# Forward transform of a Fourier and feed-forward kernel: the first stage with the input as weights on quarters of the array, the second from SBUF on row halves

## The chip, the core and the metric

The kernel runs on one core of a Trainium2 chip. The metric is the device time of one execution in microseconds (us). Engines are named as in the profile: PE (matrix engine; PEld its weight loads), DVE and ACT (the two that read PSUM), POOL, and SP, which here only issues transfers. Operands live in SBUF (128 rows), products in eight PSUM banks of 512 float32 columns, inputs and spilled tiles in DRAM (HBM).

## The reference

Two batches of 3008 positions with 256 features pass through a transform along the positions, one complex linear layer with soft shrinkage, the transform back, and two feed-forward layers. The change lies in `rfft` alone; what follows `irfft` is named as far as it shares engines with it.

```python
X = np.fft.rfft(x, axis=1)                  # x: 2 x 3008 x 256
Yr = Xr @ w_r - Xi @ w_i + b_r
Yi = Xr @ w_i + Xi @ w_r + b_i              # then soft shrinkage by 0.01
y = np.fft.irfft(Y, n=x.shape[1], axis=1)
h = x @ w_in                                # x: y as 6016 x 256; 2048 wide
x = (h * np.clip(h + 3.0, 0.0, 6.0) / 6.0) @ w_out
out = (silu(x @ w_gate) * (x @ w_val)) @ w_out2   # 1536 wide
```

## The kernel before

3008 is split into 47 x 64. The first stage (`pre`, L324) takes transforms of 47 points over positions 64 apart; only 24 of the 47 results are wanted, each with a real and an imaginary part (48 numbers). The second stage (`s2`, L398) takes transforms of 64 points, four of the 24 groups at a time: a block (b, Q) is batch b and group four Q = 0..5. ORDER (L490) lists the twelve blocks, batch 0 first, and p counts them; batch 1 begins at p = 6.

**First stage before.** x lies in eight rooms of 94 used rows (two neighbouring positions times 47, padded to 96, spread over 128 rows from the second room on, the rest set to zero), 2048 columns each. A table `fwd1_sb` of 96 columns stands as weights, and `pre(n)` streams two times 512 columns of a room past it, n = 0..7 for batch 0 and 8..15 for batch 1; ACT and DVE each copy one result (L341, L343) to SBUF. From there it is written to DRAM (`Bd`, eight transfers on POOL's queue, one on ACT's, the others on SP's), and `load_q` (L388) reads it back with (part, position) on the rows as z, one transfer of 512 KB for each block, three buffers.

**Second stage before.** For each block and each half dh of the 256 features, `s2` multiplies four times: weights z (128 x 128), 128 moving columns of the table m (L405). `S(p)` is the pair of these halves; ACT and DVE make from each a high part, a low part, and the sum of the parts the same way (L411 to L419).

**The order.** `seq` (L510 to L531) is a hand-written list of steps; every engine works through its own instructions in that order. It begins with `prepare` (constants, the linear layer's weights `lin`, split into high and low parts during `pre` 6 to 10 by the steps of `amid`), goes on with `pre` 0 to 12, S(0) and `pre` 13, and then runs over p: L(p), the linear layer of block p, in two halves `ln` (L436) of one L456 and 18 products each; S(p+1) ahead; A(p-1), the first stage back (`ia`, L474, products on row halves of the array, L481), whose result POOL's queue writes to `Cd`. `pre` 14 and 15 stand in p = 1 and 2. Each half of L(1) to L(7) also does one step of `conv1` (L206), which turns 64-bit weights into high and low parts on ACT and DVE, with one load of 256 KB on SP's queue. At p = 8 `post` (L587) computes the last stage back for the first tokens, on quarters of the array (L584: 48 rows, 64 columns of weights, up to 47 moving columns), and from there on `unit` (L658), the first feed-forward layer, stands between the pieces of L, S and A. What comes after p = 11 is feed-forward work.

At the start four products of zeros (L271) on quarters of the array run before the first data has come. `load_x` (L244) and `load_m` (L384) put their transfers on SP's queue, which issues in order: a transfer that waits for its buffer holds up what stands behind it.

## Time and profile before

| what | us |
|---|---|
| median of 3 runs | 1136.46 |
| range of the runs | 1136.12 to 1137.76 |
| the profiled execution | 1135.67 |
| span within it (first to last instruction) | 1133.9 |
| PE busy in the span | 1124.4 |
| DVE busy | 913.4 |
| ACT busy | 779.3 |
| POOL busy | 48.5 |

Busy time is the time in which an instruction of the engine is under way; instructions of one engine overlap in it, so the distance from one start to the next says what one costs in a dense row. The chain that ended last is followed back from the last instruction, at each step to what released it. A float32 product of PE stands in the trace as two instructions, a product of rounded float32 (fp32r) as one.

### The profile page before, as it was taken

To read this page: it belongs to the slowest core of one execution; us is meant where nothing else is said; L and a number is where in the kernel's file an instruction comes from. 1 tells how busy PE (TensorE), PEld (TensorE's weight loads), DVE (VectorE), ACT (ScalarE), POOL (GpSimd) and SP (SyncE) were. 2 spreads that over 40 slices of the span, in tenths; PEclk is the share of its full clock that TensorE was granted. 3 is DMA by queue.
4 is the path that set the end of the run, shared out by engine and by line. 5 is a ranking of instruction groups with operands and counts; after the bars stand their busy time and mean duration, and the time that the engine had idled before them with its cause. 6 is when DMAs were issued, how large, how long until landed. Compare 5 with 4: busy or idle time off the path is not lost.

```text
span 1133.9 us, 18058 instructions
## 1 busy us (share of the span) xinstructions
PE 1124.4 (99%) x6576; PEld 979.9 (86%) x6576; DVE 913.4 (81%) x1629; ACT 779.3 (69%) x1432; POOL 48.5 (4%) x79
## 2 busy tenths in 40 slices
PE   9999999999999999999999999999999999999998
PEld 3898888888888888888899888888888888888997
DVE  5688996899999999999988777777777777777665
ACT  3677876688788788787787666666666666666655
POOL 4000004500000000000000000000000000000000
PEclk9999999999999999999999999999999999999999
DMA  8997534964473664554543544644644644644552
GB/s 304 335 317 229 182 97 146 297 240 172 135 252 110 197 223 153 183 200 149 209 177 126 195 166 167 241 167 168 241 167 168 241 167 168 237 168 167 208 205 75
DMA packets 70185, 219.65 MB, mean 194 GB/s; under 512 B 6688, under 2 KB 30272, under 8 KB 58368
## 3 DMA queue, kind: packets, MB, share of 16 engines
q1 hardware_dynamic: 67280, 208.76, 53.3%
q0 software_dynamic: 2496, 9.05, 2.1%
q8 instruction: 52, 0.85, 0.3%
q10 hardware_dynamic: 320, 0.69, 0.2%
q14 instruction: 37, 0.30, 0.1%
HBM read 172.07 MB, written 46.40 MB: 193 GB/s over the span
## 4 chain that ended last, share of the span: by engine, by line
PE 86%; DVE 8%; ACT 4%; issue 2%; DMA 1%; SPq 0%; DVEq 0%; ACTq 0%
PE acc L136 11%; PE acc L138 11%; PE acc L137 11%; PE P L945 8%; PE P L947 8%; PE P L946 8%; PE Tb L947 4%; PE Tb L945 4%; PE Tb L946 4%; PE p L339 2%; PE Q L945 2%; PE Q L947 2%; PE Q L946 2%; DVE r L993 2%; DVE gated L141 1%
## 5 line engine op out<-in xcount | busy, mean ns | idle before, releaser
L1002 ACT COPY hold<-P 128x512 f32<-128x512 f32 (+1 forms) x224 | 128.4, 573 | 57.3 <-PE P L947 55.8
L624 ACT CAST gated<-r 128x512 fp32r<-128x512 f32 (+1 forms) x160 | 98.4, 615 | 65.1 <-DVE r L993 63.6
L141 DVE TENSOR_TENSOR gated<-s,gated 128x512 fp32r<-128x512 f32 (+1 forms) x144 | 97.5, 677 | 49.9 <-ACT gated L1129 49.7
L141 DVE TENSOR_TENSOR gated<-r,gated 128x512 fp32r<-128x512 f32 (+1 forms) x160 | 108.1, 676 | 21.8 <-ACT gated L624 17.3
L136 PE MATMUL acc<-gated,w_o 128*128 128x512 f32 (+1 forms) x320 | 120.4, 376 | 0.0
L137 PE MATMUL acc<-gated,w_o 128*128 128x512 f32 (+1 forms) x320 | 119.6, 374 | 0.0
L138 PE MATMUL acc<-gated,w_o 128*128 128x512 f32 (+1 forms) x320 | 119.6, 374 | 0.0
L997 DVE TENSOR_TENSOR hold<-Q,hold 128x512 f32<-128x512 f32 (+1 forms) x112 | 75.9, 678 | 43.4 <-ACT hold L1002 41.8
L138 PE MATMUL acc<-gated,slot 128*128 128x512 f32 (+1 forms) x288 | 108.1, 375 | 0.0
L136 PE MATMUL acc<-gated,slot 128*128 128x512 f32 (+1 forms) x288 | 108.0, 375 | 0.1
L137 PE MATMUL acc<-gated,slot 128*128 128x512 f32 (+1 forms) x288 | 107.9, 375 | 0.0
L997 DVE TENSOR_TENSOR hold<-P,hold 128x512 f32<-128x512 f32 (+1 forms) x112 | 75.8, 677 | 33.6 <-PE P L947 33.6
L1169 ACT ACTIVATE s<-hold 128x512 f32<-128x512 f32 (+1 forms) x72 | 45.0, 624 | 81.0 <-DVE hold L997 81.0
L989 ACT ACTIVATE r<-hold,consts 128x512 f32<-128x512 f32 (+1 forms) x120 | 85.7, 714 | 14.4 <-DVE hold L997 12.4
L945 PE MATMUL P<-xo,slot 128*128 128x512 f32 (+1 forms) x240 | 90.2, 376 | 1.7 <-DVE hold L997 1.2
L1129 ACT CAST gated<-s 128x512 fp32r<-128x512 f32 (+1 forms) x144 | 87.8, 610 | 4.4 <-DVE s L1184 4.2
L947 PE MATMUL P<-xo,slot 128*128 128x512 f32 (+1 forms) x240 | 88.8, 370 | 0.0
L946 PE MATMUL P<-xo,slot 128*128 128x512 f32 (+1 forms) x240 | 88.8, 370 | 0.0
L997 DVE TENSOR_TENSOR hold<-Tb,hold 128x512 f32<-128x512 f32 (+1 forms) x112 | 75.9, 678 | 14.2 <-PE Tb L947 10.4
L993 DVE SCALAR_TENSOR_TENSOR r<-r,hold 128x512 f32<-128x512 f32 (+1 forms) x120 | 81.0, 675 | 2.5 <-ACT r L989 1.6
L1174 ACT ACTIVATE s<-hold 128x512 f32<-128x512 f32 (+1 forms) x72 | 45.0, 625 | 45.2 <-DVE hold L997 45.2
L1002 ACT COPY hold<-Tb 128x512 f32<-128x512 f32 (+1 forms) x112 | 65.2, 582 | 4.0
(190 smaller groups left out, 2847.1 us busy)
## 6 DMA issues: line engine op xcount, KB each, us to landing
slot<-Wd SPq DMA_DIRECT2D x72, 1152.0 KB
slot<-Sd SPq DMA_DIRECT2D x40, 896.0 KB
st<-in_w SPq DMA_DIRECT2D x68, 256.0 KB
Wd<-slot SPq DMA_DIRECT2D x12, 1152.0 KB
z<-Bd SPq DMA_DIRECT2D x12, 512.0 KB
Cd<-cs POOLq DMA_DIRECT2D x12, 512.0 KB, 3.4
Xd<-x SPq DMA_DIRECT2D x20, 256.0 KB
raw<-Xd SPq DMA_DIRECT2D x5, 1024.0 KB
```

What stands on the lines that cost most here:

```text
L136: nc.tensor.matmul(o, wl, xh, start=start, stop=False)
L137: nc.tensor.matmul(o, wh, xh, start=False, stop=False)
L138: nc.tensor.matmul(o, wh, xl, start=False, stop=stop)
L141: nc.vector.tensor_tensor(out=o, in0=full, in1=hi.bitcast(F32), op=ALU.subtract)
L624: nc.scalar.copy(hi[:, :n], g[:, :n])
L945: nc.tensor.matmul(o, wl, hi, start=start, stop=False, skip_group_check=not start)
L946: nc.tensor.matmul(o, wh, lo, start=False, stop=False, skip_group_check=not start)
L947: nc.tensor.matmul(o, wh, hi, start=False, stop=True, skip_group_check=not start)
L993: nc.vector.scalar_tensor_tensor(out=r[:, :n], in0=r[:, :n], scalar=6.0, in1=x[:, :n], op0=ALU.min, op1=ALU.mult)
L997: nc.vector.tensor_tensor(out=h, in0=x[:, :n], in1=c, op=ALU.add)
L1002: nc.scalar.copy(c, x[:, :n])
L1129: nc.scalar.copy(hi[:, :nb], t[:, :nb])
```

## The change

In `pre` the input itself is now the weights: for each feature, half and position block, 64 columns of x (47 rows) are loaded into one quarter of the array, and the table `fwd1_sb` (47 x 48) streams past. Four quarters take turns, two PSUM tiles collect eight features each (results 8 columns apart), and one copy of 384 columns on ACT and one on DVE move them to z in SBUF, which holds a whole batch and has one buffer. The result already has (half, position) on the rows, so the way through DRAM (`Bd`, `load_q`, `write_second`, `group`) goes. `s2` multiplies on row halves, 64 rows for each dh, twice as many products, real and imaginary part added up in PSUM; the table m has its 64 rows twice and twice the columns, in two buffers instead of three. All eight `pre` of batch 0 stand at the start, followed by S(0) and S(1); those of batch 1 stand in p = 4 and 5. x comes in four rooms a batch with 48 rows for each row half (47 and one of zeros), so the memsets of the rooms go; batch 1's rooms are loaded at the ends of p = 0 to 3. `lin` moves from POOL's queue to SP's. Four more products of zeros, 320 columns wide, stand at the start. From p = 8 on two units stand at the end of a step that were on both sides of S's halves.

The diff, cut where the code before shows what goes:

```diff
-    fwd2 = np.zeros((NG, 2, 2, NJ, 2, K2))
+    fwd2 = np.zeros((NG, 2, NJ, 2, 2, K2))
...
-    fwd2 = fwd2.reshape(NG, 128, 128).transpose(1, 0, 2).reshape(128, NG * 128)
+    fwd2 = fwd2.reshape(GC, K2, 128).transpose(1, 0, 2).reshape(K2, GC * 128)
+    fwd2 = np.concatenate([fwd2, fwd2])
...
-    both = np.zeros((128, 2 * GW))
-    mixed = fwd1.reshape(QP, NG // 4, 16).transpose(0, 2, 1).reshape(QP, GW)
-    both[:QP, :GW] = mixed
-    both[::2, GW:], both[1::4, GW:] = mixed[:64], mixed[64:]
-    inv2 = np.zeros((128, QP))
-    inv2[:48, :N1] = inv2[64:112, :N1] = f.transpose(2, 1, 0).reshape(48, N1)
-    out = {"fwd1": both, "inv2": inv2, "fwd2": fwd2, "inv1": inv1}
+    fwd1, inv2 = np.zeros((128, 64)), np.zeros((128, 96))
+    for r in (0, 64):
+        fwd1[r : r + N1, :GC] = f.reshape(N1, GC)
+        inv2[r : r + GC, :N1] = f.transpose(2, 1, 0).reshape(GC, N1)
...
-    Bd = [dram.tile([16 if n < NQ else GW, NJ * DIM], F32, name=f"Bd{n}") for n in range(NQ + 1)]
...
-    NT = NJ // 4
-    TC = 4 * DIM
-    room = {}
+    NT, ND = 8, 8
+    TC = 2 * ND * K2
 
     def ring4(name):
-        return ap_.tile([128, 4 * DIM], F32, tag="bc", name=name, bufs=4)
-
-    def load_x(k):
...
-    room[5] = xs_p.tile([128, 3 * TC], F32, tag="gs", name="room5", bufs=1)[:, : 2 * TC]
-    room[6], room[7] = room[0], room[1]
+        return ap_.tile([128, 4 * DIM], F32, tag="bc", name=name, bufs=2)
+
+    first = w1p.tile([128, NT * TC], F32, tag="w1_o", name="first", bufs=1)
+    room = {(0, k): first[:, 2 * k * TC : 2 * (k + 1) * TC] for k in range(4)}
+
+    def load_x(b, k, c=slice(0, 2 * TC)):
+        for r in range(2):
+            nc.sync.dma_start(room[b, k][64 * r : 64 * r + GC, c], x[b, k, r, :, c])
+
+    for c in (slice(0, TC // 2), slice(TC // 2, TC), slice(TC, 2 * TC)):
+        load_x(0, 0, c)
+    nc.scalar.dma_start(fwd1_sb, fwd1)
 
     p = [psf[0]([128, 512], f"p0_{n}") for n in range(2)]
-    for r, c, n in ((0, 0, 0), (64, 64, 0), (0, 64, 1), (64, 0, 1)):
-        nc.tensor.matmul(p[n][c : c + 64], zeros[r : r + 64, :64], zeros[r : r + 64], start=True, stop=True,
-                         tile_position=(r, c))
+    for n in (512, 320):
+        for r, c in ((0, 0), (64, 64), (0, 64), (64, 0)):
+            nc.tensor.matmul(p[r // 64][c : c + 64, :n], zeros[r : r + 64, :64], zeros[r : r + 64, :n], start=True,
+                             stop=True, tile_position=(r, c))
...
-        lin_st = ap_.tile([128, 2, 2, DIM], F32, tag="z", name="lin_st", bufs=3)
+        lin_st = ring4("lin_st").rearrange("p (k a b) -> p k a b", k=2, a=2)
         b_st = spread("b_st")
-        nc.gpsimd.dma_start(lin_st, lin)
+        load_x(0, 1)
+        nc.sync.dma_start(lin_st, lin)
+        load_x(0, 2)
+        load_x(0, 3)
+        load_m(0, 0)
         nc.gpsimd.dma_start(b_st[:64], bias)
-        for h in range(2):
-            nc.gpsimd.memset(room[5][:, h * TC : (h + 1) * TC], 0.0)
-        load_x(5)
-        load_m(0, 0)
...
         amid.update({
-            6: [lambda: mixed(ALU.subtract), lambda: hi(2, 0)], 7: [lambda: mixed(ALU.add), lambda: hi(0, 2)],
-            8: [lambda: lo(2, 0), lambda: shifts(0)], 9: [lambda: lo(0, 2), lambda: hi(1, 3)],
-            10: [lambda: lo(1, 3), lambda: shifts(1)]})
+            4: [lambda: mixed(ALU.subtract), lambda: hi(2, 0)], 5: [lambda: mixed(ALU.add), lambda: hi(0, 2)],
+            6: [lambda: lo(2, 0), lambda: hi(1, 3), lambda: shifts(0)],
+            7: [lambda: lo(0, 2), lambda: lo(1, 3), lambda: shifts(1)]})
 
...
-    first = w1p.tile([128, NT * TC], F32, tag="w1_o", name="first", bufs=1)
-    second = w1p.tile([128, 5 * TC], F32, tag="w1_g", name="second", bufs=1)
-
-    def pre(n):
-        sent()
-        b, i = divmod(n, NT)
+    def pre(b, i):
+        src = room[b, i // 2][:, i % 2 * TC : (i % 2 + 1) * TC]
+        if i == 0:
+            z_t[b] = ap_.tile([128, GC, 128], F32, tag="z", name=f"z{b}", bufs=1)
+        p = [psf[0]([128, 512], f"p1_{b}_{i}_{r}") for r in range(2)]
+        for n in range(ND):
+            for r, c in ((0, 0), (1, 1), (0, 1), (1, 0)):
+                k, e = slice(64 * r, 64 * r + N1), slice(64 * c, 64 * c + 64)
+                at = 128 * n + 64 * c
+                nc.tensor.matmul(p[r][e, n : n + ND * (GC - 1) + 1 : ND], src[k, at : at + 64], fwd1_sb[k, :GC],
+                                 start=True, stop=True, tile_position=(64 * r, 64 * c))
+        for r, copy in enumerate((nc.scalar.copy, nc.vector.tensor_copy)):
+            at = 64 * r + ND * i
+            copy(z_t[b][:, :, at : at + ND], p[r][:, : ND * GC].rearrange("p (a n) -> p a n", n=ND))
         if b == 0:
-            o = first[:GW, i * TC : (i + 1) * TC]
-        elif i < 4:
-            o = second[:GW, i * TC : (i + 1) * TC]
...
-
-    bview = [t.rearrange("(g w) (j d) -> (w j) g d", w=4, j=NJ) for t in Bd]
+            for g in amid.pop(i, ()):
+                g()
+
...
     def load_m(b, Q):
         if (b, Q) not in m_t:
-            m_t[b, Q] = table("m", fwd2, Q, f"m{b}_{Q}", 3)
-
-    def load_q(b, Q):
...
-            nc.tensor.matmul(p[:, g, :], z_t[b, Q][:, g, dh * 128 : (dh + 1) * 128], m_t[b, Q][:, g, :],
-                             start=True, stop=True)
+            m_t[b, Q] = table("m", fwd2, Q, 8, f"m{b}_{Q}")
+
+    def s2(b, Q):
+        flush()
+        t = ap_.tile([128, 2, 2, 3, 4 * K2], F32R, tag="X", name=f"X{b}_{Q}", bufs=2)
+        X[b, Q] = [t[:, k] for k in range(2)]
+        p = [psf[0]([128, 4, 128], f"p2_{b}_{Q}_{dh}") for dh in range(2)]
+        for i in range(8):
+            for dh in range(2):
+                r = slice(64 * dh, 64 * dh + 64)
+                nc.tensor.matmul(p[dh][:, i // 2], z_t[b][r, 8 * Q + i], m_t[b, Q][r, i], start=i % 2 == 0,
+                                 stop=i % 2 == 1, tile_position=(64 * dh, 0))
+        for dh in range(2):
+            evict(b, Q, dh, p[dh])
+
+    def evict(b, Q, dh, p):
...
-    def ahead(p):
-        if p < len(ORDER):
-            load_q(*ORDER[p])
-
     def S(p):
-        def first():
-            ahead(p + 1)
-            s2(*ORDER[p], 0)
-        return [first, lambda: s2(*ORDER[p], 1)] if p < len(ORDER) else []
+        def both():
+            if p + 1 < len(ORDER):
+                load_m(*ORDER[p + 1])
+            s2(*ORDER[p])
+        return [both] if p < len(ORDER) else []
 
...
-    P = [lambda n=n: pre(n) for n in range(NB * NT)]
-    seq = [prepare] + P[:NT] + [lambda: load_q(0, 0)] + P[NT : NT + 1]
-    seq += [lambda: group(1, nc.scalar)] + P[NT + 1 : NT + 2] + [lambda: load_q(0, 1)]
-    seq += P[NT + 2 : NT + 5] + S(0) + P[NT + 5 : NT + 6]
-    rest = P[NT + 6 :]
+    P = [[lambda b=b, i=i: pre(b, i) for i in range(NT)] for b in range(NB)]
+
+    def load_next(k):
+        if k == 0:
+            t = w1p.tile([128, 5 * TC], F32, tag="w1_g", name="second", bufs=1)
+            room.update({(1, i): t[:, 2 * i * TC : 2 * (i + 1) * TC] for i in range(2)})
+        elif k > 1:
+            room[1, k] = xs_p.tile([128, 2 * TC], F32, tag="xa", name=f"room{k}", bufs=2)
+        load_x(1, k)
+
+    seq = [prepare] + P[0] + S(0) + S(1)
     for p in range(len(ORDER)):
-        l, a = L(p), A(p - 1)
-        some = [rest.pop(0) for _ in range(p in (1, 2))]
+        l, a, s = L(p), A(p - 1), S(p + 1) if p else []
         u = [lambda: unit()] if p >= FROM else []
-        head = l[:1] + ([lambda: post(0, 0), lambda: post(0, 1)] if p == FROM else [])
-        s = S(p + 1)
-        if p == NQ:
-            seq += head + s[:1] + a + s[1:] + l[1:]
+        if p == FROM:
+            seq += l[:1] + [lambda: post(0, 0), lambda: post(0, 1)] + u + s + a + u + l[1:] + u + u
+        elif p == NQ - 2:
+            seq += l[:1] + s + a + P[1][:2] + l[1:] + P[1][2:4]
+        elif p == NQ - 1:
+            seq += l[:1] + P[1][4:] + s + a + l[1:]
         else:
-            seq += head + u + some + s[:1] + u + s[1:] + a + u + l[1:] + u
-        seq += [sent]
-        if p in (2, 3):
-            seq += [lambda i=p - 2: write_second(i)]
+            seq += l[:1] + u + s + a + u + l[1:] + u + u
+        if p < 4:
+            seq += [lambda k=p: load_next(k)]
...
-    xp = x.reshape(NB, N1, NJ, 2, DIM).transpose(0, 3, 1, 2, 4).reshape(NB, QN, NJ * DIM)
-    xp = np.pad(xp, ((0, 0), (0, QP - QN), (0, 0))).reshape(NB, QP, NJ // 8, 8 * DIM).transpose(0, 2, 1, 3)
+    xp = np.zeros((NB, 4, 2, GC, 32 * K2), np.float32)
+    xp[:, :, :, :N1] = x.reshape(NB, N1, K2, 2, 2, 4, 16).transpose(0, 5, 4, 1, 6, 3, 2).reshape(NB, 4, 2, N1, 32 * K2)
```

## Rows read from the trace of the kernel before

**Rows 1.** The page: PE's busy time, and the chain that ended last.

```profile
...
PE 1124.4 (99%) x6576; PEld 979.9 (86%) x6576; DVE 913.4 (81%) x1629; ACT 779.3 (69%) x1432; POOL 48.5 (4%) x79
...
PE 86%; DVE 8%; ACT 4%; issue 2%; DMA 1%; SPq 0%; DVEq 0%; ACTq 0%
...
```

**Rows 2.** Busy time in four stretches; columns in the first line.

```profile
...
core 0: us, PE busy (x) PEld busy (x) DVE busy (x) ACT busy (x) POOL busy (x), PEclk, DMA share, GB/s
4.10:33.30 29.20, 29.19 (x73) 11.98 (x73) 14.97 (x25) 11.94 (x23) 9.96 (x17) 1.00 0.87 321
33.30:68.20 34.90, 34.90 (x274) 30.63 (x273) 24.89 (x51) 23.20 (x53) 3.25 (x6) 1.00 1.01 353
68.20:101.90 33.70, 33.70 (x282) 31.01 (x281) 29.10 (x69) 24.72 (x61) 1.62 (x3) 1.00 0.71 226
101.90:166.00 64.10, 63.22 (x555) 56.41 (x554) 60.36 (x147) 48.59 (x111) 2.13 (x4) 1.00 0.58 182
...
```

**Rows 3.** PE timeline at the start: start, length in us, line, operation.

```profile
...
1.52 1.99 PE L272 MATMUL p<-zeros 64*64 64x512 f32 x8 [1.52 <-DVE zeros L230]
...
4.11 7.05 PE L337 MATMUL p<-room,fwd_sb 96*96 96x512 f32 x8 [0.60 <-DMA room<-in_x]
...
11.00 3.17 PE L339 MATMUL p<-room,fwd_sb 128*96 128x512 f32 x7
...
```

**Rows 4.** PE groups by form, 0 to 200 us: busy us, mean ns.

```profile
...
L339 PE MATMUL p<-room,fwd_sb 128*96 128x512 f32 x56 | 24.7, 592 | 0.0
...
```

**Rows 5.** Timeline of PE, 33 to 102 us, as rows 3.

```profile
...
32.98 0.78 PE L456 MATMUL p<-shift,ones 128*128 128x512 f32 x1
...
43.56 2.01 PE L405 MATMUL p<-m,z 128*128 128x128 f32 x16
...
63.73 0.28 PE L405 MATMUL p<-m,z 128*128 128x128 f32 x1
63.94 2.00 PE L481 MATMUL p<-yp,n 64*128 64x256 f32 x16
...
72.30 2.00 PE L481 MATMUL p<-yp,n 64*128 64x256 f32 x16
...
99.58 0.48 PE L456 MATMUL p<-shift,ones 128*128 128x512 f32 x1
...
101.91 0.38 PE L456 MATMUL p<-shift,ones 128*128 128x512 f32 x1
...
```

**Rows 6.** Timeline of PE at the last stage back.

```profile
...
104.82 1.50 PE L584 MATMUL p<-inv_sb,ct 48*64 48x47 f32 x88 [0.28 <-DMA ct<-Cd]
...
```

**Rows 7.** Stretches as rows 2; last two columns DMA share, GB/s.

```profile
...
0.00:5.00 5.00, 2.87 (x9) 0.70 (x10) 3.31 (x6) 1.28 (x1) 4.47 (x9) 1.00 0.55 161
5.00:8.00 3.00, 3.00 (x5) 1.09 (x4) 0.15 (x1) 0.58 (x1) 2.94 (x4) 1.00 0.95 298
8.00:11.00 3.00, 3.00 (x5) 0.85 (x3) 0.54 (x1) 0.58 (x1) 2.80 (x7) 1.00 0.98 396
11.00:13.00 2.00, 2.00 (x6) 0.81 (x5) 0.77 (x2) 0.58 (x1) 0.80 (x2) 1.00 1.01 410
...
35.00:70.00 35.00, 35.00 (x276) 30.82 (x276) 24.40 (x50) 23.53 (x53) 3.25 (x6) 1.00 1.01 353
...
```

**Rows 8.** DVE timeline at 73 us, 256 and 512 columns.

```profile
...
72.70 0.41 DVE L413 TENSOR_TENSOR sum<-p,sum 128x256 f32<-128x256 f32 x1
73.03 0.68 DVE L141 TENSOR_TENSOR X<-p,X 128x512 fp32r<-128x512 f32 x1
73.63 0.68 DVE L470 SCALAR_TENSOR_TENSOR yp<-yb,yc 128x512 f32<-128x512 f32 x1
...
```

**Rows 9.** Groups: copies of the first stage, DVE and ACT.

```profile
...
L343 DVE COPY first<-p 96x512 f32<-96x512 f32 x8 | 5.5, 687 | 11.4 <-PE p L337 5.8 <-PE p L339 5.6
...
L341 ACT COPY first<-p 96x512 f32<-96x512 f32 x8 | 4.7, 582 | 14.0 <-PE p L339 7.1 <-PE p L337 6.9
...
```

**Rows 10.** Waits of SP queue to 110 us: total, times, longest.

```profile
...
SPq L174 <- DVE wt L188: 22.7, 7, 5.3
...
```

## The prediction

> **What bounds the kernel now.** I read the page first: PE is busy 99% of the span and the chain that ended last lies 86% on PE [rows 1]. A busy PE need not be a full one, so the second view is the busy time by stretch: from 4.1 to 101.9 us PE is busy without a gap, from 101.9 to 166 for all but 0.9 us [rows 2], while DVE needs 29.1 of 33.7 us at most before 101.9. In this part of the kernel every microsecond of PE work that goes is therefore a microsecond of the span, until DVE, a transfer or a wait ends last instead. Third, the start of the PE timeline [rows 3]: eight L337 instructions take 7.05 us, 0.85 us from one to the next, and right behind them, from 11.0 us, L339 goes on with the same 512 columns every 0.43 us (seven in 3.17 us, the last of which alone lasts 0.59). [...]

> The steady period comes from a later stretch of the PE timeline: A(p) (L481) starts at 63.94 and at 72.30, so one step of the loop over ORDER takes 8.36 us [rows 5]: twice L (99.58 to 101.91, 2.33 each), one S and one A. L(0) counts from 33.4 us (its L456 starts at 32.98 behind the last `pre` and lasts 0.4 longer than the one at 101.91), L(8) from 101.91 [rows 5]. Between them lie eight steps, 68.5 us: the first without an A (6.2), steps 1 and 2 with a `pre` of four times 0.43 each (10.1), the others 8.36, the last of them 8.6.

> **The first stage.** Removed: 32 products of 512 columns, 8 instructions at the lower level (6.9 us) and 56 [rows 4] at 0.43 (24.0 us): 30.9 us of PE. Added: 16 `pre` with 32 products each on quarters of the array, 64 trace instructions (a float32 product is two). The row for this shape is L584, the last stage, which has the same weights (48 rows x 64 columns, new for each product), the same four quarters in turn and 47 columns instead of 48: 88 instructions in 1.50 us, the last of which lasts 0.23 [rows 6], so 14.6 ns apart. One `pre` is 64 x 14.6 = 0.93 us at the upper level and, taken as twice that, 1.87 at the lower. What no row shows is a PSUM write in steps of 8 columns; the bounds are no cost (an L's 18 products of 256 columns each write every second column, and with one of 512 take 2.33 us [rows 5], 0.12 each) and twice the time (+0.93 a `pre`); I take no cost, as the nearer row.

> [...]

> *Batch 0, from the start to L(0).* Transfers: x comes in four rooms of 0.79 MB, `lin` (0.52) now sits on the SP queue between the first two and the last two, then m (0.52). With the rates of before (161 GB/s to 5 us, 298 to 8, 396 to 11, 410 to 13 [rows 7]; sums 0.81, 1.70, 2.89, 3.71 MB) the rooms are there at 5.0, 7.7, 11.1 and 13.0 us and m at 14.3. The four dummies of 512 columns end at 3.5 us [rows 3]; four more of 320 columns add two instructions of 0.53: PE is free for `pre` at 4.4. At the lower level until 11.0: `pre` 0 to 2 end at 10.0, the fourth at 11.4; then 0.93 each: 4 and 5 end at 13.3, 6 and 7 (last room) at 15.1. DVE: copies of 384 columns lie between 256 (0.33) and 512 columns (0.60 from start to start [rows 8]; 0.69 is the length of one copy of 512, ACT's 0.58 [rows 9]), so 0.47. In the last four `pre` DVE also does five operations of 512 columns, one short and one more of 0.6 for `lin` and `shift` (some 3.9 us); up to the copy of the last `pre` four copies, three long ones and the short one: 4 x 0.47 + 3 x 0.6 + 0.33 = 4.0, begun at 12.4: 16.4 us. So S(0) waits for DVE, not for PE or m. S(0): 16.5 to 18.4, S(1) behind it. X(0) is complete enough for L(0) some 2.5 us after S(0) ends (both halves now end together, so ACT's first copy and four DVE operations, 2 x 0.33 + 2 x 0.6, stand behind it): L(0) at **21.0**, 12.4 us earlier than before. The memsets of the rooms, the writes to Bd and the reads of z go; POOL and ACT's queue lose them and nobody waits for either here.

> **The second stage.** Before: 8 products of 128 columns a step, 16 instructions in 2.01 us, of which the last lasts 0.28 [rows 5]: 0.115 apart, 1.85 in all. After: 16 products with 64 rows, 32 instructions, two side by side on row halves. L481 shows what row halves give: 16 instructions with twice the columns (256) take 2.00 us [rows 5], which is eight pairs of 0.22, where one after another they would take 3.4. With 128 columns a pair is 0.11: 16 pairs 1.78 us. Entering row halves costs about 0.1 (L405 at 63.73, next due 63.84, L481 at 63.94), which A(p), now right behind S, no longer pays: **0** in sum. Bounds: -0.1 a step, and +1.78 if weights of 128 columns for the two halves load one behind the other (L481 leaves 0.22 for both, so it can't exclude that); I take 0, because L584 loads four sets of 64 columns in 4 x 14.6 = 58 ns, which one after another would not fit where load and matmul of 128 columns on the full array come every 0.115. Evictions are the same instructions.

> **Batch 1, in steps 4 and 5.** Four `pre` in each: 3.7 us of PE and 0.3 for three changes of tiling. Step 4: 8.36 + 4.0 = 12.4. In step 5 the four stand right before S(6), which needs all of z, one buffer now; it waits for the last copy (0.47 and what DVE has queued): +0.7, so 13.1. Behind S(6) on PE stand A(4) and the second half of L(5). The copies write z after S(5) has read it, which PE has done by then. DVE gets 4 x 0.47 in each step, beside some 29.1/33.7 x 8.36 = 7.2: 9.1 of 12.4, still hidden. Steps 1 and 2 lose their `pre` (-1.75 each), step 0 its S (-1.75), which stands before L(0).

> **Queues.** SP loses 12 z loads, six writes and the wait for them, gets 8 loads of x at the ends of steps 0 to 3, `lin`, and m at twice the bytes. m has two buffers: m(p+2) waits for S(p), which is over when it is asked for, but for m(2) at the start, behind which n(0) and x of batch 1 stand, wanted 8 us later or more. SP's long waits (L174 for DVE, up to 5.3 us [rows 10]) stay. Bytes in steps 1 to 3: x 0.79, m 0.52, n 0.26, two weight pieces 0.52, Cd 0.52 = 2.6 MB in 8.36 us, 312 GB/s, under the 353 that flowed from 35 to 70 us [rows 7]. So no transfer ends last.

> **Sum.** L(0) 21.0; steps 0 to 7: 4.5 + 3 x 8.36 + 12.4 + 13.1 + 8.36 + 8.6 = 72.1 (before 68.5); L(8) at 93.1 instead of 101.9: 8.8 us less. Behind it the order only has two units side by side where S parted them; PE is dense there, so 0. The profiled execution took 1135.67 us (span 1133.9), which gives 1126.9; the median shown, 1136.46, is 0.8 above it, so **1127.5** for a median.

> **The rivals.**
> 1. *The clock stays low through the small matmuls.* Before, it rose under dense full-array work; here the first stage has 47 rows on quarters and pauses. For it: L337 ran 6.9 us at the lower level though PE was dense. Against: L584 kept the upper one, and the dummies are longer. Then the eight `pre` end at 19.4, S(0) runs from 20.0 at half speed to 23.7, L(0) begins at 26.5 and spends some microseconds at half speed, as if begun at 29: 8 us lost, **1135**, no change.
> 2. *Slower: weights of the two row halves load one after the other.* A pair of S is 0.22, S is 3.56: 12 x 1.78 = 21.4 us more, **1149**. It decides from a pair of 0.17 on (8.8 us over 12 x 16 pairs is 46 ns more than 0.11).
> 3. *Small products with results 8 columns apart start further apart than L584's.* At the bound of twice, 0.93 more for the 8 `pre` of batch 1 and for the five of batch 0 that run at the upper level: 12 us, **1139**. The rows of L (every second column, full pace) and of L584 speak against it. [...]
> 4. *The gain is hidden in part*: copies with short runs are slow, or DVE's backlog holds S(0), S(6) and the steps between: 2 us each at two or three places: **1132**.
> 5. *More*: x faster than before's ramp (even 48-row transfers) and the clock up sooner; then DVE's 4.0 starts 2 to 3 us earlier: **1124**.

> **How the numbers follow.** Forecast 0.66 (1123 to 1131), rival 1 0.13 (1130 to 1137), 2 0.07, 3 0.03, 4 0.08, 5 0.03. Range 1122 to 1136: it leaves out rivals 2 and 3, rival 1's upper end and the tails of the rest. 0.2% (2.3 us) is about what a measurement can tell from no change: faster is the forecast with 4 and 5 and a third of 1, 0.81; same is the rest of 1 and part of 3, 0.10; slower is 2, part of 3 and a tail, 0.09.

> **What would show it.** First L456 near 21 us, L(8)'s near 93; `pre` at 0.93 us once the clock is up and the first matmuls every 29 ns until then; S at 1.8 to 2.0 us; steps of 8.36 with 12 to 13 us at 4 and 5; no PE idle over 1 us but before S(0), L(0) and S(6). [...]

## The result and the profile after

The changed kernel takes 1150.71 us in the median of 4 runs (1149.44 to 1152.41) against 1136.61 (1136.12 to 1137.76): ratio 1.0124, 95% interval 1.0106 to 1.0141. It is 1.2% slower; the forecast was 0.8% faster, and the range ended at 1136. The profiled execution took 1151.74 us (span 1149.9), 16.07 more than the one before.

The page still shows PE at 98% of the span and PE as 90% of the chain that ended last, but with 1160 matmuls, and as many weight loads, more. The new figure is the line PEclk, tenths of full speed in slices of 28.7 us: the granted clock is low in slices 1, 2 and 4. q8 (kind `instruction`) brings PE's instructions, as its count says: 61 packets, 1.00 MB, for 15472 matmuls and weight loads, about 254 to a packet (before, 52 and 0.85 MB for 13152, 253 to a packet).

```profile
PE 1126.4 (98%) x7736; PEld 999.1 (87%) x7736; DVE 908.5 (79%) x1626; ACT 775.9 (67%) x1432; POOL 35.5 (3%) x62
...
PEclk6897999999999999999999999999999999999999
...
q8 instruction: 61, 1.00, 0.4%
```

The PE timeline of the changed kernel at the start (start, length in us, line, operation, count, and in brackets the idle time before and what ended it; L249 are the dummies, L307 `pre`, L335 S, L390 the first product of a half of L). It answers [rows 3].

```profile
1.52 3.05 PE L249 MATMUL p<-zeros 64*64 64x512 f32 x16 [1.52 <-DVE zeros L222]
4.35 2.02 PE L307 MATMUL p<-fwd_sb,first 47*64 47x48 f32 x64
6.57 0.31 PE L307 MATMUL p<-fwd_sb,first 47*64 47x48 f32 x2 [0.20 <-DMA first<-in_x]
7.47 1.14 PE L307 MATMUL p<-fwd_sb,first 47*64 47x48 f32 x62 [0.59 <-DMA first<-in_x]
10.00 0.45 PE L307 MATMUL p<-fwd_sb,first 47*64 47x48 f32 x2 [1.39 <-DMA first<-in_x]
12.16 2.37 PE L307 MATMUL p<-fwd_sb,first 47*64 47x48 f32 x77 [1.72 <-DMA first<-in_x]
17.01 4.13 PE L307 MATMUL p<-fwd_sb,first 47*64 47x48 f32 x127 [2.48 <-issue]
25.46 5.26 PE L307 MATMUL p<-fwd_sb,first 47*64 47x48 f32 x178 [4.32 <-issue]
31.50 6.25 PE L335 MATMUL p<-m,z 64*128 64x128 f32 x64 [0.77 <-ACT z L311]
37.67 0.48 PE L390 MATMUL p<-shift,ones 128*128 128x512 f32 x1
```

Two kinds of idle time: for x (`DMA first<-in_x`, 3.9 us in four rows) and, larger, `issue`, where PE waited for nothing that the profile shows (6.8 us). Counted as the prediction counts it (the first product of L(0) starts at 37.67 and lasts 0.1 longer than in a dense row), L(0) is at 37.8 us, where 21.0 was forecast and 33.4 was before: 16.8 us of miss.

From there the steps 1 to 3 are the old ones (they end at 50.59, 58.95 and 67.31: 8.36 each). Step 4, with four `pre`, is 12.48; the timeline shows them at 2.08 us for two, and S at 2.06:

```profile
69.63 2.06 PE L335 MATMUL p<-m,z 64*128 64x128 f32 x32
...
73.34 2.08 PE L307 MATMUL p<-fwd_sb,second 47*64 47x48 f32 x128
```

Step 5, with the same four `pre`, takes 21.5 us instead of 13.1 (79.79 to 101.3). The chain of what ended last there (start, length, what):

```profile
80.60 0.11 PE p L385
80.72 2.22 issue
82.94 0.38 PE p L386
...
84.32 0.11 PE p L387
84.59 0.22 PE p L386
...
85.02 7.08 PE p L307 x256
...
92.78 3.79 PE p L335 x32
96.57 2.54 PE p L415 x16
```

The next two steps end where L(8) begins (timeline):

```profile
101.33 0.38 PE L390 MATMUL p<-shift,ones 128*128 128x512 f32 x1
...
118.05 0.38 PE L390 MATMUL p<-shift,ones 128*128 128x512 f32 x1
```

Step 5 has a stop of 2.22 us in the middle of L; then the products of L go from 0.11 to 0.22 us at 84.4, and all that follows takes nearly twice its length: 1.77 us per `pre`, S 3.79, A 2.54. Steps 6 and 7 are 8.36 again. L(8) starts at 118.05 instead of 101.91 [rows 5], 16.1 us later, which is the whole difference between the two profiled executions. So two places hold the miss of 25 us: 16.8 up to L(0), and 8.4 in step 5.

Busy time by stretch (columns in the first line; the last three are granted clock, DMA share and GB/s) shows the clock at its lower level (0.50 of full speed; the upper one is 1.00, and its records have no other) from 10 to 30 us (it came back at 36.6), and again for parts of 80 to 100; before, its first record is a rise to 1.00 at 11.0 us, where 512 columns go from 0.85 to 0.43 us [rows 3], and it has no fall within the span. The line of 10 to 20 us has the other surprise: the DMA engines are busy all the time (1.04) with 207 GB/s, where a share of 1.01 stood beside 410 and 353 before [rows 7].

```profile
core 0: us, PE busy (x) PEld busy (x) DVE busy (x) ACT busy (x) POOL busy (x), PEclk, DMA share, GB/s
...
10.00:20.00 10.00, 5.77 (x177) 5.32 (x179) 1.11 (x2) 0.96 (x2) 0.00 (x0) 0.50 1.04 207
20.00:30.00 10.00, 5.68 (x205) 5.49 (x202) 3.38 (x6) 2.99 (x6) 0.00 (x0) 0.50 0.39 114
...
80.00:90.00 10.00, 7.78 (x207) 7.34 (x210) 4.79 (x10) 3.11 (x8) 0.00 (x0) 0.72 0.15 55
90.00:100.00 10.00, 9.25 (x133) 8.53 (x129) 3.07 (x6) 3.50 (x8) 0.00 (x0) 0.60 0.01 2
```

**Three theories** come out of this. *A, transfers:* 48 neighbouring rows are filled at about half the rate of rows spread over all 128. *B, instructions:* a `pre` uses up 64 matmuls and 64 weight loads in a microsecond, faster than they are brought to PE. Between the stops at 14.53 and 21.14 PE ran 127 matmuls and 127 weight loads (a few records can be missing), about 256 instructions; counted in PE's stream the stops at 14.53, 21.14 and 80.72 lie ahead of instructions 450, 706 and 2498, which is 256 and 7 x 256 apart. *C, clock:* products on quarters of the array do not hold the clock at its upper level (rival 1 of the prediction). The rival of each theory is that the other two explain the loss without it.

### The profile page after: what moved, and what is told of

Its sections match the earlier page's. It is cut to its first block, busy times and chain, and to the rows that moved or that the text cites. A ratio compares the mean times of both kernels' runs of the same rounds, so it can differ in the third digit from the quotient of the medians.

```text
span 1149.9 us, 20296 instructions
## 1 busy us (share of the span) xinstructions
PE 1126.4 (98%) x7736; PEld 999.1 (87%) x7736; DVE 908.5 (79%) x1626; ACT 775.9 (67%) x1432; POOL 35.5 (3%) x62
## 4 chain that ended last, share of the span: by engine, by line
PE 90%; DVE 5%; ACT 2%; issue 2%; DMA 1%; SPq 0%; DVEq 0%; ACTq 0%
PE acc L130 12%; PE acc L128 12%; PE acc L129 12%; PE P L882 8%; PE P L884 8%; PE P L883 8%; PE Tb L882 4%; PE Tb L883 4%; PE Tb L884 4%; PE Q L883 2%; PE Q L884 2%; PE Q L882 2%; PE p L335 2%; PE p L307 2%; PE p L415 1%
## 5 line engine op out<-in xcount | busy, mean ns | idle before, releaser
L926 ACT ACTIVATE r<-hold,consts 128x512 f32<-128x512 f32 (+1 forms) x120 | 85.5, 713 | 14.5 <-DVE hold L934 12.4
```

Of the source, the lines that this page charges most:

```text
L926: nc.scalar.activation(r[:, :n], x[:, :n], AF.Relu, bias=three)
```

## The experiments

The first kernel measures the three disputed things by themselves, with none of the real work.

> The whole computation is left out; the kernel measures the disputed costs by themselves. First six sets of four transfers with 8 KB a row, each set begun when the one before has landed: near48 (48 neighbouring rows, at 0 and at 64 in turn, as the changed kernel loads x), near64 (64 neighbouring rows), wide48 and wide64 (every second row), all128, and pair48 (as near48, the two halves on two queues). Theory A, that a transfer into one half of the rows reaches only half of the way into SBUF: near48 and near64 flow at about 200 GB/s, wide48, wide64 and all128 at about 400, pair48 at over 300. Rival, that 48 rows are too few for a transfer: near48 and wide48 both slow, near64 and wide64 both faster. Then twelve `pre` of quarter products from data at rest, back to back, without a copy or a transfer; eight more with two full-array products of 512 columns behind each; and twelve with eight transfers under way. Theory B, that PE's instructions arrive 256 at a time and that this takes some 3.6 us: the twelve take 1.8 us each, with a stop of about 1.7 us behind every 128 products if the clock is at its upper level; none in the eight with full products; longer stops with transfers under way. Rival, that PE was held by data alone: 0.93 us each without a stop. Theory C, that quarter products do not hold the upper clock level: the granted clock falls to 0.5 within the twelve and comes back with the full products. Rival: it fell only for the idle time, and stays at 1.0 here.

Its transfers came in groups of four, each alone. Row by row: 48 neighbouring rows (rows 0 to 47 and 64 to 111 in turn), 64 neighbouring rows, 48 and 64 rows in steps of two, all 128 rows, and 48 neighbouring rows with the two halves on two queues. The last column is the rate:

```profile
4.00:12.00 8.00, 0.00 (x0) 0.00 (x0) 0.00 (x0) 0.00 (x0) 1.00 0.83 136
16.00:24.50 8.50, 0.00 (x0) 0.00 (x0) 0.00 (x0) 0.00 (x0) 1.00 0.91 200
28.00:32.50 4.50, 0.00 (x0) 0.00 (x0) 0.00 (x0) 0.00 (x0) 1.00 1.01 279
36.50:40.80 4.30, 0.00 (x0) 0.00 (x0) 0.00 (x0) 0.00 (x0) 1.00 0.97 402
45.00:53.00 8.00, 0.00 (x0) 0.00 (x0) 0.00 (x0) 0.00 (x0) 1.00 1.02 429
57.00:64.00 7.00, 0.00 (x0) 0.00 (x0) 0.00 (x0) 0.00 (x0) 1.00 0.86 176
```

Neighbouring rows get half the rate of spread ones at the same size (200 against 402, 136 against 279). That is A, as a rate; that a half of the rows has only half of the way into SBUF is not shown. Its figures for 48 rows did not come, though, and its rival holds in part: 48 rows have a lower rate than 64 in both patterns. They land as late as 64 (8.0 and 7.8 us in the median for neighbouring rows, 5.3 and 5.3 for spread ones), so a quarter fewer bytes buy nothing. A second queue helped little (176 against 136, where over 300 was expected).

Then came the quarter products of `pre`: twelve in a row, eight with two full products behind each, twelve in a row again. The eight transfers meant for the last twelve ran beside the first twelve instead. The chain of what ended last (L72 the quarter products, L63 full ones):

```profile
81.44 2.93 PE p L72 x189
84.37 3.67 issue
88.05 3.67 PE p L72 x128
91.71 1.44 issue
93.14 3.66 PE p L72 x128
96.80 0.62 issue
...
125.78 1.91 PE p L63 x4
...
143.10 3.98 PE p L72 x261
147.08 1.24 issue
148.31 2.08 PE p L72 x128
150.39 1.65 issue
152.04 7.11 PE p L72 x256
```

No `DMA` and no other engine stands between these products, and within a row of twelve 128 matmuls (256 instructions) lie from each stop to the next: B. The stops lie ahead of instructions 450, 706, 962, 3266 and 3522, the first two the same as in the changed kernel and all a multiple of 256 apart. At the upper level 128 matmuls last 2.08 us and the next came 1.65 later, 3.73 us for 256 instructions, two `pre`; at the lower level 128 take 3.66 us by themselves, and the last row has no stop. With transfers under way (328 GB/s from 80 to 107) the stops reached 3.67 us. With two full products behind each `pre` (115.7 to 137.8) there was no stop at all: a period of 3.0 us for 136 instructions.

The trace also has every packet of q8, each of 16384 bytes (us):

| stop begins | packet starts | packet has landed | PE goes on |
|---|---|---|---|
| parts, 147.08 | 145.62 | 146.72 | 148.31 |
| parts, 150.39 | 149.34 | 150.51 | 152.04 |
| changed kernel, 14.53 | 13.72 | 15.23 | 17.01 |
| changed kernel, 21.14 | 23.09 | 24.15 | 25.46 |
| changed kernel, 80.72 | 80.45 | 81.33 | 82.94 |

Each of these stops ends 1.3 to 1.8 us behind the landing of a packet. Without transfers the next packet starts 1.0 us after PE went on (148.31, 149.34) and the one after it 1.1 us (152.04, 153.15). In the changed kernel, with the DMA engines busy for 0.99 of the time from 17 to 23 us, it starts 6.1 us after (17.01, 23.09) and is then under way for 1.06 us: the longest stop comes from a packet that starts late, not from one that moves slowly.

C is shown in part. The clock fell 5 us after the first and 8 us after the last twelve had begun (86.4 and 151.2), stayed at 1.00 through the eight mixed ones, and rose with the full products behind the twelve. Up to 107.0 and 162.8 the quarter products ran for 9.6 and 10.8 us without a stop of more than 0.07 us, at the lower level, and did not bring the clock back. But both falls lie inside a stop, so this run does not tell whether the products or the idle time lost the clock.

Next, each cause in the kernel itself. **pad128** pads x to 64 rows a half and moves it in transfers over all 128 rows, a third more bytes:

```diff
-        for r in range(2):
-            nc.sync.dma_start(room[b, k][64 * r : 64 * r + GC, c], x[b, k, r, :, c])
+        nc.sync.dma_start(room[b, k][:, c], x[b, k, :, c])
...
-    xp = np.zeros((NB, 4, 2, GC, 32 * K2), np.float32)
+    xp = np.zeros((NB, 4, 2, 64, 32 * K2), np.float32)
```

> One change to the changed kernel: each piece of x has 64 rows for each half instead of 48 and comes in one transfer of all 128 rows, so a third more bytes. Theory A: 1.05 MB a room at 350 to 400 GB/s, the last room at 13 to 15 us instead of 20, the first L at 28 to 33 us instead of 38, and 1141 to 1147 us. Rival, that instruction supply and clock alone hold the first stage: the eight `pre` end at 30 us as before, 1150 or a little more for the bytes.

It took 1143.78 us. The first product of L(0) started at 32.2 (37.7 in the changed kernel), 5.5 us earlier, and S(0), S(1) took 5.95 us. The granted clock reads 1.00 there from 0 to 30 us, but 127 matmuls of `pre` took 3.66 us, as at the lower level in parts: its first record is a rise, at 30.8, and what lies before a first record counts as full speed. So a mean granted clock leaves out a clock that has not risen yet. In the chain the last stop of 2.24 us is still there, between 127 and 99 matmuls of `pre`:

```profile
14.27 3.66 PE p L306 x127
17.93 2.24 issue
20.17 3.35 PE p L306 x99
```

A single run is thin for 7 us, so it was timed in several.

> The kernel of pad128 once more, beside the kernel before in several runs, for an interval: one look gave 1143.78 us against 1135.46. If the transfers of neighbouring rows are worth what the look showed, the ratio to the kernel before lies at 1.005 to 1.008 (1142 to 1145.5 us) with an interval that leaves out the changed kernel's 1.0124; if the look was a lucky one, it lies at 1.010 or above.

1143.82 us (1142.86 to 1144.78), ratio 1.0057, interval 1.0042 to 1.0071, apart from the changed kernel's 1.0106 to 1.0141: A is worth 6.9 us, half of the loss of 14.1. The edit spreads the rows over all 128, but also takes 64 rows in place of 48 and one transfer in place of two; these were not taken apart. **room0** has every `pre` of batch 0 read the first room and does not load the other three:

```diff
-        load_x(0, 1)
         nc.sync.dma_start(lin_st, lin)
-        load_x(0, 2)
-        load_x(0, 3)
...
-        src = room[b, i // 2][:, i % 2 * TC : (i % 2 + 1) * TC]
+        src = room[b, i // 2 if b else 0][:, i % 2 * TC : (i % 2 + 1) * TC]
```

> One change to the changed kernel: all eight `pre` of batch 0 read the first room, and the transfers of the other three rooms of batch 0 are left out, so that x never holds PE. Theory B and C (instruction supply and clock): a `pre` still takes about 1.8 us, the eight end at 18 to 21 us, the first L is at 24 to 27 and the time 1137 to 1141. Theory A alone: `pre` at 0.93 us once the clock is up, the eight end at 12 to 14, the first L at 18 to 21, 1132 to 1135.

1142.31 us. With nearly all waiting for x gone, the eight `pre` still took 16.9 us (4.35 to 21.27, 2.1 each) and L(0) started at 27.7, 10.0 us earlier but far from the forecast 21.0: taking the transfers away alone does not bring the forecast about. **warm** looks at the other place, step 5, with three full products ahead of each `pre` of batch 1:

```diff
+        for _ in range(3 if b else 0):
+            nc.tensor.matmul(p[0], ones, shift, start=True, stop=True)
```

> One change to the changed kernel: before each `pre` of batch 1 stand three full-array products of 512 columns (0.22 us each at the upper level) whose results are overwritten. Theory C: the clock stays at its upper level through step 5, and S(6) and A(4) behind the four `pre` take 3.8 us again instead of 6.3. Theory B: the four `pre` still take 1.8 to 1.9 us each, now with stops at 256 instructions in them, and the time falls by 2 to 3 us, to 1148 to 1149. Without theory B they take 0.93 + 0.65 = 1.6 us each without a stop, and the 2.2 us stop in front of them goes as well: 1145 to 1146. If the full products hold the clock no better, nothing is gained and eight times 0.65 or more is lost: 1153 to 1156.

1151.37 us, later than expected. The two rows are steps 4 and 5, both 17.0 long and both at clock 1.00:

```profile
67.00:84.00 17.00, 16.25 (x357) 13.86 (x355) 11.77 (x27) 9.28 (x23) 0.53 (x1) 1.00 0.73 233
84.00:101.00 17.00, 16.25 (x355) 13.98 (x356) 8.28 (x18) 8.09 (x19) 0.53 (x1) 1.00 0.08 23
```

In step 5 no stop and no fall of the clock are left, and 17.0 less four fillings of 0.87 us is 13.5, against 13.1 forecast: B and C together are all that ailed it. In step 4, which had no stop, four fillings and a wait of 0.75 us for m are lost (17.0 instead of 12.5): the sum is zero.

**halves** (on pad128) is to tell B from C: `pre` on row halves, 128 columns of weights, half the instructions.

```diff
-            for r, c in ((0, 0), (1, 1), (0, 1), (1, 0)):
...
+            for r in range(2):
+                k = slice(64 * r, 64 * r + N1)
+                nc.tensor.matmul(p[r][:, n : n + ND * (GC - 1) + 1 : ND], src[k, 128 * n : 128 * n + 128], fwd1_sb[k, :GC],
+                                 start=True, stop=True, tile_position=(64 * r, 0))
```

> On top of pad128 one change: `pre` multiplies on row halves, with 128 columns of x as weights, instead of on quarters with 64, so a `pre` has 16 products and half the instructions for the same results. Theory B: no stop at 256 instructions is left in steps 4 and 5, although a pair of products with 128 columns of weights takes 0.11 us and a `pre` 1.8 us of PE instead of 0.93; steps 4 and 5 together take 32 to 34 us, as in pad128 (31.2), within 2 us. Rival, that the instructions' number does not matter and PE's own time does: 8 x 0.9 = 7 us more, 38 to 39 us. For the clock: row halves keep it up better or not, to be seen; time 1142 to 1147.

1155.98 us, far above what was expected. No stop of the kind `issue` of half a microsecond is left in steps 4 and 5, as B has it; but the clock still fell (8.7 to 36.0, 83.8 to 87.2 and 94.1 to 100.9 us), and a `pre` costs 1.84 us at the upper and 3.4 to 3.6 at the lower level, as long as its supply took before (1.87). Steps 4 and 5 took 36.6 us, between the two expectations. The falls at 83.8 and 94.1 are what C needs: PE was busy without a gap from 60 to 96.4 us, so there no idle time lost the clock. That holds for products on row halves. On quarters, every fall in these runs lies in a wait or a stop or at most 1.5 us behind one, so that quarter products alone lose it is not shown.

**split** (on pad128) only moves the `pre` of batch 1 apart: one behind S and one behind A in step 4, two ahead of A and two behind it in step 5.

```diff
-            seq += l[:1] + s + a + P[1][:2] + l[1:] + P[1][2:4]
+            seq += l[:1] + s + P[1][:1] + a + P[1][1:2] + l[1:] + P[1][2:4]
...
-            seq += l[:1] + P[1][4:] + s + a + l[1:]
+            seq += l[:1] + P[1][4:6] + a + P[1][6:] + s + l[1:]
```

> On top of pad128 one change: in step 4 A(3) stands between the first and the second `pre` of batch 1, in step 5 A(4) between its second and third. The longest run of `pre` is now two. Theory B: stops at 256 instructions shrink, since A needs 1.9 us for 32 instructions: steps 4 and 5 take 27 to 29 us instead of 31.2, 1140 to 1142. Theory C: the clock stays up in step 5. Rival, that the block's place does not matter: 1143 to 1144.

The clock stayed up through both steps, and they took 28.1 us (61.3 to 89.4) where pad128 took 31.2. The total, 1143.74, did not show the 3 us, and met the rival's figure. L(0) started at 31.3 and L(8) at 106.6, against 109.8 in pad128; but PE then waited 2.1 us for ACT in two places between 850 and 1000 us, in the feed-forward part, which pad128 does not have. **fill0** (on pad128) puts one full float32 product of 512 columns ahead of each `pre` of batch 0, and **both** is split with it:

```diff
+        if b == 0:
+            nc.tensor.matmul(p[0], first[:, :128], first[:, :512], start=True, stop=True)
```

> On top of pad128 one change: before each `pre` of batch 0 stands one full-array product of 512 columns (two instructions of 0.43 us at the upper level) whose result is overwritten. Theory C: the clock rises by 11 us and stays up, S(0) and S(1) take 3.9 us instead of 5.9, a `pre` with its filling 1.9 us as in the run with filling for batch 1, and the first L starts at 25 to 28 us instead of 32: 1137 to 1140. If full products do not raise it there, each filling costs 1.7 us: the first L at 36 or later, 1147 or more.

> Both of the last two changes on top of pad128: the sum of the two gains by theories B and C, 6 to 10 us, gives 1134 to 1138, about the kernel before.

fill0 took 1141.58, above what was expected: the clock was up from 7.2 us through S(0) and S(1), which took 3.84 us instead of 5.95, and L(0) started at 30.0 though the eight fillings cost 8.5. both took 1140.43, also above, with the clock up from 5.4 us to the last products, and stops of 1.02, 1.46 and 1.79 us left. Two kernels have a smaller filling than both, 256 and 128 columns in place of 512:

> The last kernel (128-row transfers of x, filling in batch 0, A between the `pre` of batch 1) with the filling halved to 256 columns, 0.43 us of PE at the upper level instead of 0.85. Theories B and C: a `pre` with its filling falls from 2.1 to 1.85 us, what 132 instructions take to arrive; the clock stays up; the first L starts at 26 to 28 us instead of 30 and the time is 1136 to 1139. If instruction supply is no bound, 1.6 us each: 25 us or less, 1134 to 1135. If half the filling does not hold the clock, S(0) and S(1) take 5 us or more again, 1141 to 1144.

> The same with 128 columns of filling, 0.21 us. Theory B: no gain over 256 columns, since instructions arrive no faster, 1136 to 1139; theory C: this is the one that may lose the clock in batch 0, then 1141 to 1144.

In the profiled runs of these the clock fell, at 14.7 us just behind a stop and at 8.6 us just behind a wait for x, and L(0) started at 34.0 and 33.9. fill256 took 1145.8 us (1143.91 to 1150.21, ratio 1.0097, interval 1.0073 to 1.0121), fill128 1144.59. Then both was timed in several runs.

> The kernel of both once more, for an interval: one look gave 1140.43 us against 1136.47. The theory of three causes (transfers, instruction supply, clock) with two of them taken away expects 1139 to 1142 us, a ratio of 1.003 to 1.005 whose interval lies above 1, below pad128's: what is left are the stops for instructions and the filling. The rival, that the clock costs nothing of its own and the look was scatter, expects the same ratio as pad128 in the same call, within 0.1%.

This was a miss for the larger part of the expectation: 1145.54 us (1138.25 to 1150.93 in ten runs), ratio 1.0074, interval 1.0051 to 1.0096, not below that of pad128. In the profiled one of these runs the clock fell at 21.3 us, behind a stop, and two fillings and two `pre` ran at half speed (chain, as above; L303 the filling, L308 `pre`):

```profile
18.09 0.24 PE p L308 x3
18.33 1.46 issue
19.79 1.14 PE p L308 x61
20.92 1.64 PE p L303 x2
22.56 1.89 PE p L308 x64
24.46 2.00 PE p L303 x2
```

Within these ten runs the mean granted clock goes with the time: 1138.25, 1141.56 and 1143.10 us at 0.999 to 1.000, 1143.07 at 0.997, 1145.42 to 1149.44 at 0.992 to 0.996, 1150.93 at 0.989. At half speed 0.011 of 1149 us is some 25 us of low clock, so by this estimate up to 12.6 us of loss, as much as the whole spread. Elsewhere it does not go with the time: a run of fill256 at 1.000 took 1146.13 us, and pad128 took 1142.86 and 1144.00 at 0.998, 1143.63 and 1144.78 at 0.988. So for this kernel it is likely, and not shown, that the clock makes the spread. Its three runs at 0.999 to 1.000 still lie above the 1137.12 us (1135.69 to 1138.39) of the kernel before, timed beside it. No version beat it.

## Why the prediction was wrong

**What held.** PE sets the end in this part: L(8) later by 16.1 us made the execution longer by 16.07. The later starts of pad128, room0 and warm come out in their times as well (L(8) 7.9, 6.6 and 15.7 us later, executions 8.1, 6.6 and 15.7 longer); in the kernels both, fill0 and split 0.6, 1.6 and 3.4 us came on top. Steps 1 to 3, 6 and 7 are 8.36 (8.6 forecast for the last), step 4 is 12.48 (12.4 forecast), and a `pre` takes 0.93 us at the upper level where its instructions are there (2.08 for two, of which the last product is 0.22). The second stage on row halves costs nothing: S is 2.06 us, less the 0.28 of its last product and over 16 pairs 0.11 a pair, and rival 2 falls. Results in steps of 8 columns cost nothing, so rival 3 falls too. Step 5 without supply stops and at the upper level is 13.5 (13.1), as warm showed.

**What failed first: "With the rates of before" the "rooms are there at 5.0, 7.7, 11.1 and 13.0 us".** Most of these rates were read from transfers of every second or fourth of the 128 rows and carried to transfers of 48 neighbouring rows. PE waited for x at 6.9, 8.6 and 10.4 us, and the last room came at about 20 us. parts gave the rates and pad128 the worth of the other layout, 6.9 us of the median. Rival 5 even called the new transfers faster. In parts 64 neighbouring rows got 200 GB/s and 64 spread ones 402; why is not shown.

**What failed second: 64 x 14.6 ns for one `pre` after another.** The row for it [rows 6] was right about the array, and one such row of 88 matmuls cannot show what it takes to feed PE: its 176 matmuls and weight loads are fewer than one block of 256, and it has no stop. A `pre` is 128 instructions, sixteen of them 2048. Their supply takes 3.73 us for 256 (parts), 1.87 us a `pre`, twice the price in the sum, and more while transfers run. In the changed kernel this was 2.48 and 4.32 us ahead of L(0) and 2.22 in step 5. The packets of q8 show that beside transfers a block starts late (6.1 us after PE went on, 1.0 without transfers); what holds its start was not measured. With two full products behind each `pre` no stop was left (parts, 115.7 to 137.8), and none over 0.07 us in a row of `pre` at the lower level without transfers (parts, from 152.04); in rows of `pre` at the upper level or beside transfers a block of 256 cost a stop of up to 4.32 us.

**What failed third: the clock, rival 1, at a chance of 0.13.** The rival named the right thing, a low clock in the first stage, but saw too little of it in two ways. It held the clock to be late at the start (before, it rose at 11.0 us); in fact it rose at 5.9 us, fell at 9.3 while PE waited for x, and came back only at 36.6 near the end of S(1), so that S(0), S(1) took 6.2 us instead of 3.9. And nothing in the prediction had it fall again in step 5 (84.4 to 98.0, 1.4 us behind the stop there), where the four `pre` took 7.08 us instead of 3.7, S(6) and A(4) 6.3 instead of 3.7. The argument against it was that L584 kept the upper level; those 1.5 us stand between full products, the eight `pre` stand alone, with waits and stops between them. parts shows both cases.

The losses by supply and by the clock cannot simply be added: at the lower level two `pre` take 3.66 us, at the upper one their supply takes 3.73. So for a row of `pre` alone the clock hardly matters; it costs in the products of S, A and L behind them. Of the 16.8 us up to L(0), the transfers hold 5.5 (pad128) and up to 10.0 (room0, which has nearly none to wait for and less traffic beside the supply); the other 6.8 are, by what is left, supply and clock. How these 6.8 divide stays open: no kernel took the supply away at the start without adding work.

## What to carry to other kernels

Count the instructions of a step as well as its columns: products so small that 256 instructions pass in 2 us were paced here by their supply and not by the array (2.08 us of products in 3.73, parts), and a price read from a short row of them held only for a short row (14.6 ns from one to the next in a row of 88 [rows 6], 29.1 over the 128 of these 3.73 us). Put such products one or two at a time between longer ones that the kernel has anyway, not eight in a row: split left stops of 0.34 us and no fall of the clock in its two steps. Filling that does no work gained nothing clear here: warm took 1151.37 us against 1150.71, and the interval of both is not below that of pad128. When a transfer is given other rows, take its rate from a row with the same pattern of rows, not from one with the same bytes (200 and 402 GB/s for the same 512 KB in parts).
